# A planned attention and gated-FFN kernel: fillers, transfer rates and the order of the work set anew

## The chip, the cores and the metric

One core of a Trainium2 chip runs the whole program. The metric is the device time of one execution in microseconds (us), from start to end, as the median of several runs. The core has a matrix engine (TensorE, PE in the profile; PEld is its loading of weights), a vector engine (VectorE, DVE), a scalar engine (ScalarE, ACT), a general engine (GpSimd, POOL) and a queue for transfers (SyncE, SP). Each takes its instructions in the order of the program and waits at semaphores for the others. Transfers go through 16 DMA engines; they are issued here by GpSimd, SyncE and ScalarE.

## What is computed

Attention without softmax over 8 batches of 12 heads, 448 positions and 64 values a head, and then a gated feed-forward block over the 3584 resulting rows:

```python
scores = scale * np.matmul(q, k.transpose(0, 1, 3, 2))
attn = np.maximum(scores, 0.0) ** 2 / S
attn_out = np.matmul(attn, v)

x = attn_out.transpose(0, 2, 1, 3).reshape(B * S, H * D)   # 3584 x 768
g = x @ w_gate                                             # 768 x 1536
gelu = 0.5 * g * (1.0 + erf(g * inv_sqrt2))
out = (gelu * (x @ w_val)) @ w_out                         # 1536 x 768
```

Inputs and output are float32 in memory; the kernel computes in bfloat16 with float32 sums.

## The kernel before

**Tiles.** TensorE is used as four 64 x 64 quarters. Nearly every product is a matmul of 64 x 64 weights with up to 448 columns, and one instruction of the plan is a pair of them on one half of the rows: the lists `PE0` and `PE1` hold the pairs of the two halves, and both run at the same time. A batch has six pairs of heads, and its work is cut in three thirds of four heads. For a third, `load_qk` brings queries and keys (`qk16`), which are turned: for batches 0 and 1 and one third of batch 2 by transposes on TensorE against a unit matrix `ident` (`add_first_transposes`, `add_transposes`) and a copy to `qkT`, for all others by a transposing DMA from SyncE (`add_dma_transposes`). Then seven score units a third, 21 a batch (`add_scores`): a score product into a PSUM tile `sp` (there are two), relu by ScalarE into `attnT` (line 757), and the square by VectorE (line 766). `add_values` multiplies `attnT` with the values `v16` into a bank `ff`, copied as `xT`. The feed-forward part takes `xT` with the gate and value weights `wg0` to `wg5`, `wv0` to `wv5` (each 256 of the 1536 columns) either plainly (`add_gate_value`) or, for two batches at a time, with sums of tiles and seven products in place of eight (`add_pair`); the result `uT` goes through the output weights `wo`, also with seven products (`add_product`), into `osb`, and from there to memory (`emit_store`).

**Order.** None of the order is left to a scheduler at run time. While the program is built, `run_plan` plays through a model of the engines: every step is an `Op` with a cost, the steps that it depends on, and a `lag`; at each turn the one that can start first is emitted. For TensorE the order is mostly given from outside. The string `LINE` lists the units after the first batch (`s` is a score unit, `o` a value unit, a digit a gate or value product of that batch, three letters like `2F6` a pair product, two like `b2` an output product), `LOADS` lists the loads on GpSimd's queue after the first batch (`w`, `o`, `q`, `v`), and the numbers `SPOTS`, `FIRSTS`, `PLACE5`, `TURNS` and `SOON` set the places of the first batch's steps, which `work` holds with a time each.

**Loads in the plan.** `load` gives each transfer a time, its bytes in float32 by a rate: 300e3 bytes per us for the first batch, 400e3 after it, 385e3 for weights, all times `SLOW` = 1.06, one after the other, landing 2 us after their end. What waits for one waits for a margin as well: `LATE` = 1.0 us for weights and for batches 1 and 2, `LATER_BY` = 3.0 us for all later ones.

**Fillers.** In the first `FILL` = 30 us the function `fill` is told of each stretch in which the plan has TensorE idle. It puts matmuls of 512 columns of a zero tile (`held`, line 611) there, as many as 0.22 us each fit, into a bank `ff` whose last reader is done. A bank that was not yet used at all is not in `held` and is not taken.

**The end.** The last of 14 groups of output rows makes two row tiles, `t0` and `t1`, in halves of 384 columns. The last two stores of whole rows (`t1`) both go to SyncE's queue; the half rows of `t0` go one to SyncE and one to ScalarE each time.

Of the kernel before, what the change touches and what calls it, by code (L numbers as in the profile page):

```python
# [8 lines left out]


LINE = """
b2 0E1 0 s 2F6 1 s 2B1 3 s 2E6 o 1 a7 o s 1 0F7 0 0 2 s s s 0 s 0F1 j6 3 h1 0F3 0E5 0 s 0 o o a2 s
s a4 s o 0 0F5 3 b1 s c1 3 0E2 0 0 c5 2A1 s 0F6 1 o 0 0E7 o s 0 0 2A3 2 1 2E1 2F7 o 1 d4 s 0 2 0 1
s s 2B7 s a6 2B2 s s s 2D6 2B6 2D1 2 6J4 s s 2A2 4 i1 4C1 1 0E4 s 0F4 0 j5 3 o o a1 4D1 1 b3 s o
2B5 1 g2 o 0 0E6 a3 2A5 s s 0 1 s 1 o c6 s 1 0F2 s s s s 1 s 1 2A6 o s 1 0 s 2F1 2D4 1 o s s o 2F3
a5 s 2D2 s s d1 b5 2F5 1 g7 s 1 s 6B4 s 2A7 0E3 s s s 2D3 s s 1 s 4F1 b6 2 2A4 s c7 2 2 s s s s 2C4
d5 4A5 o o b7 c4 s 2 s 2 s s o s 2D7 s c3 h5 2B3 b4 2C1 s 2C2 3 s 5 2B4 4E3 s 4F3 s 4A4 c2 o 2 s
6I6 d7 2C3 s s 2F2 2E7 2D5 4E1 s s k3 s o o 3 s 2C5 d6 s 3 s s 4 2E4 6K1 n5 s 6F4 2F4 o h6 2C6 f4 s
s e3 f1 2E2 2C7 s s e6 e2 d3 3 3 4A2 s 4A1 o s 2E3 2 4C3 f7 s 4 e7 s 2E5 e1 4D2 o o s o e4 2 s g6 s
d2 f3 f5 e5 4D4 3 f2 s s s s s g1 6H2 6D1 6D4 3 5 s o 6A4 h3 k7 o 4F2 o 4 4B1 s 4 s o s s 4 6B6 s s  # L20
n4 6J7 4C4 f6 s 4B3 s 4 4D3 s 4F5 g4 s g5 s o 4F6 5 4D6 s s g3 6B7 4A7 s 4E6 4A3 4C2 4 4B5 s 4A6
6D2 s s 4D7 s o o 6E1 4F7 j4 h7 s 4C5 4C7 4B7 4B6 s o 4B2 6I5 s s o 5 s s l6 s 4 j2 4B4 4C6 4 4 s o
6I7 4E2 s l3 s 4D5 4 s m3 s 5 s s 4E7 6L4 s o s 6G1 m7 h2 4E4 6A1 s 4F4 o s o 6D7 5 n3 s 4E5 6J5
6C6 6D5 6A2 s s j1 6L1 s 6A6 s 6H7 5 5 j7 6B1 i7 s 6B2 5 o s 5 6I1 i5 5 6I2 s 6H5 s m4 h4 6B3 s 6D3
5 s s 6G7 s i2 n6 6L7 s i3 s 6E7 6F7 6C5 s i6 m6 s j3 6B5 s s 6E2 6J6 i4 6C1 s 6K6 o 6A7 k1 6K7 6K3
l5 6A5 6G4 6C3 6C7 6J1 6A3 6E3 6E6 6C2 6L2 6H4 6H3 l1 m5 6D6 6C4 6I4 l7 6F3 n1 6G2 6E4 6H1 6L3 k5
6F1 m1 6F2 6G3 6F5 k6 6I3 6K2 m2 6J2 6E5 6L6 6F6 l4 6H6 k4 6G6 6G5 6K4 n7 6K5 6J3 l2 n2 k2 6L5
# [289 lines left out]
def kernel(  # L317
# [10 lines left out]
    nc = tc.nc  # L328
# [5 lines left out]
    B, H, S, D = q.shape  # L334
# [33 lines left out]

    NP = 3
    NP2 = 1  # L370
# [71 lines left out]
    def load(nbytes, emit, deps=(), cost=0.7, rate=400e3):  # L442
        def paced():
            ins = emit()
            for d in op.behind:
                tc.add_manual_dep(ins.ins, d.ins.name, SYNC, reason="pace")
            if turned:
                tc.add_manual_dep(ins.ins, turned[-1].ins.name, SYNC, reason="pace")
            loaded.append(ins)

        op = Op("POOL", cost, paced, deps)
        op.behind = [*deps]
        arrivals[op] = nbytes / rate
        op.margin = LATE if late_loads else 0.0
        POOL.append(op)
        return op

    def load_w12(i):
        cols = slice(i * WCH, (i + 1) * WCH)

        def emit(wt, src):
            return nc.gpsimd.dma_start(
                wt[:, :, :], src[:, cols].rearrange("(c p) f -> p c f", p=128))
        w12_op[i] = [load(4 * d_model * WCH, lambda wt=wt, src=src: emit(wt, src), rate=385e3)
                     for wt, src in ((wg[i], moe_w_gate), (wv[i], moe_w_val))]

    def load_wo(i):
# [6 lines left out]
    def load_qk(b, i, h0, h1, deps=()):  # L474

        src = (q, k)[i]
        m, r0 = divmod(h0, 4)

        def tile_of():
            if (b, m) not in qk16:  # L480
                pool, tag = (lpool, "qkr") if (b, m) in STAGED else (hpool, "qk16")
                qk16[b, m] = pool.tile([128, 4, SC * D], bf16, name="qk16", tag=tag)
            return qk16[b, m][HALF[i], r0:r0 + h1 - h0, :]

        op = load(4 * (h1 - h0) * S * D, lambda: nc.gpsimd.dma_start(  # L485
            tile_of(), src[b, h0:h1].rearrange("h (p c) d -> p h (c d)", c=SC)),
            deps, rate=400e3 if b else 300e3)
        qk_loads.setdefault((b, m), []).append(op)
        for pr in range(h0 // 2, h1 // 2):
            head_op[b, pr, i] = op  # L490

    def load_v(b, h0, h1, deps=()):

        m = h0 // 4
        for i in range(2):
            def emit(i=i):
                if (b, m) not in v16:
                    v16[b, m] = qkv.tile([128, 4, VC, D], bf16, name="v16", tag="v16")
                c0 = i * (SC - VC)
                return nc.gpsimd.dma_start(  # L500
                    v16[b, m][HALF[i], :, :, :],
                    v[b, h0:h1].rearrange("h (p c) d -> p h c d", c=SC)[:, :, c0:c0 + VC, :])
            op = load(4 * (h1 - h0) * VC * P * D, emit, deps, rate=400e3 if b else 300e3)
# [93 lines left out]
    def fill(t0, t1):  # L597

        if t1 > FILL or t0 <= warm_op.end:
            return  # L600
        at_rest = {k: -1.0 if r is None else r.end for k, r in held.items() if r is None or r.end is not None}
        if not at_rest:
            return
        k = min(at_rest, key=lambda k: at_rest[k])
# [1 line left out]
        n = int((t1 - t0 - 0.15) / 0.22)  # L606
        if n < 1:
            return
        t = new_bank(k, held[k])
        for _ in range(n):  # L610
            nc.tensor.matmul(t[:, :], warm[:, 0:128], warm[:, :], start=True, stop=True)  # L611

# [594 lines left out]
    def add_product(at, gr, name, final):  # L1207
# [94 lines left out]
        def emit_store(j, engine=nc.sync, part=slice(0, d_model)):  # L1302
            b, c = chunks[t % 2][j]
            rows = out[b * S:(b + 1) * S, :].rearrange("(p c) d -> c p d", c=SC)
            engine.dma_start(rows[c, :, part], osb[t][HALF[j], part])

        if name in "2345":
            st["done", t] = [*st.get(("done", t), ()), *reads]
            if final and t == t0:
                SP.append(Op("SP", 0.6, lambda: emit_store(0, nc.sync, cols), reads, prio=-1))  # L1310
                ACT.append(Op("ACT", 0.5, lambda: emit_store(1, nc.scalar, cols), reads, prio=-1))
                SP[-1].stored = ACT[-1].stored = 0.25
            elif len(st["done", t]) == 2:
                queues = (SP, "SP", 0.6, nc.sync), (ACT, "ACT", 0.5, nc.scalar)
                if final:
                    queues = queues[:1] * 2
                stored[t] = []
                for j in range(2):
                    (pool, name_, cost, engine), spare = queues[:: -1 if j and gr >= FINAL - 2 else 1]
# [262 lines left out]
```

## Time and profile before

| | us |
|---|---|
| median of 3 runs (397.22 to 400.9) | 399.4 |
| the profiled execution | 401.4 |
| its span, first to last instruction | 399.6 |
| matmuls of TensorE, all shapes (8412), time in which one runs | 389.6 |
| weights loaded into TensorE | 339.9 |
| VectorE busy | 317.6 |
| ScalarE busy | 255.7 |
| GpSimd busy | 95.0 |

A line of the profile names an engine, a line of the kernel, an operation, what it writes and reads (out<-in), a shape, and a count. In lists in order of time the first two numbers are the start and the duration, and the brackets at the end say how long the engine sat idle before it, and what it waited for. In rows by stretches the name of the engine is left out where one was asked for: length, busy time and count, then the TensorE clock that was granted (1.00 is full), the mean share of the DMA engines, and GB/s. Most matmuls are on line 422, a helper, so that they are told apart by their tiles. Line numbers of the changed kernel are 3 to 10 higher.

### The profile page before, as it was taken

The numbers are of one execution on the slowest core, as the hardware profiler recorded it, in microseconds if no ns is written. First come the engines' busy times: TensorE is split into PE (matmuls) and PEld (weight loads), VectorE is DVE, ScalarE is ACT, GpSimd is POOL, SyncE is SP. The second block draws the span as 40 slices with busy tenths as digits, with TensorE's granted clock in tenths as the row PEclk, the third lists the DMA queues.
The fourth block names the chain that finished last, engine by engine and source line by source line (L and its number), as shares of the span: only waits on it lengthen the run. The fifth ranks groups of instructions, "written<-read, shape, count | busy, mean of one in ns | idle before, by whom it ended". The sixth has DMA issues, their size and how long they took to land.

```text
span 399.6 us, 18511 instructions
## 1 busy us (share of the span) xinstructions
PE 389.6 (97%) x8412; PEld 339.9 (85%) x8412; DVE 317.6 (79%) x553; ACT 255.7 (64%) x388; POOL 95.0 (24%) x140
## 2 busy tenths in 40 slices
PE   6999999999999999999999989999999999999994
PEld 2456888888998999899999979999999988778994
DVE  3795896798896687979986778998988898768742
ACT  3876884587887657567667667678877455554310
POOL 8747042052050130310300401311110023631000
PEclk9999999999999999999999999999999999999998
DMA  7999995789698795775769968737623230000046
GB/s 103 194 200 198 197 169 81 124 105 194 97 163 125 125 178 105 99 106 77 90 105 179 147 150 167 108 66 104 75 30 82 62 102 3 3 2 3 23 117 184
DMA packets 75055, 44.39 MB, mean 111 GB/s; under 512 B 34400, under 2 KB 71520, under 8 KB 74976
## 3 DMA queue, kind: packets, MB, share of 16 engines
q0 software_dynamic: 38784, 24.39, 45.0%
q1 hardware_dynamic: 35712, 17.83, 23.2%
q8 instruction: 66, 1.08, 1.1%
q10 hardware_dynamic: 480, 0.98, 0.7%
q14 instruction: 13, 0.11, 0.1%
HBM read 48.76 MB, written 11.01 MB: 150 GB/s over the span
## 4 chain that ended last, share of the span: by engine, by line
PE 96%; DMA 1%; issue 1%; POOL 0%; DVE 0%; ACT 0%; POOLq 0%
PE ff L422 85%; PE sp L422 9%; PE ff L611 1%; DMA qk<-in_k_dram 1%; PE sp L690 1%; PE ff L690 1%; POOL qk L485 0%; DVE osb L1296 0%; ACT osb L1295 0%; POOLq L1566 0%
## 5 line engine op out<-in xcount | busy, mean ns | idle before, releaser
L757 ACT ACTIVATE attnT<-sp 128x896 bf16<-128x896 f32 x168 | 151.9, 920 | 55.0 <-PE sp L422 53.1
L422 PE MATMUL ff<-xT,wg 64*64 64x448 bf16 x1680 | 172.6, 349 | 0.0
L422 PE MATMUL ff<-xT,wv 64*64 64x448 bf16 x1056 | 115.0, 349 | 0.0
L422 PEld LDWEIGHTS <-wv 64*64 64x64 bf16 x1680 | 100.3, 106 | 10.1 <-issue 0.4
L422 PEld LDWEIGHTS <-wg 64*64 64x64 bf16 x1680 | 98.3, 106 | 9.1 <-issue 0.3
L766 DVE TENSOR_TENSOR attnT<-attnT 128x1792 bf16<-128x1792 bf16 (+1 forms) x98 | 92.0, 953 | 11.0 <-ACT attnT L757 10.7
L422 PE MATMUL ff<-attnT,v 64*64 64x448 bf16 (+1 forms) x768 | 84.0, 326 | 1.3 <-issue 1.0
L422 PE MATMUL sp<-qkT 64*64 64x448 bf16 (+1 forms) x768 | 75.1, 330 | 1.2 <-issue 0.6
L422 PEld LDWEIGHTS <-s 64*64 64x64 bf16 x1200 | 71.3, 107 | 1.5
L422 PE MATMUL ff<-ts,wv 64*64 64x448 bf16 x624 | 71.7, 349 | 0.0
L422 PEld LDWEIGHTS <-uT 64*64 64x64 bf16 x912 | 54.8, 107 | 0.9
L500 POOL DMA_DIRECT2D v<-in_v_dram x48 | 29.7, 630 | 108.4 <-DMA qkT<-qkr 41.6
L422 PE MATMUL ff<-ts,ws 64*64 64x448 bf16 x480 | 55.0, 349 | 0.0
L995 DVE TENSOR_TENSOR part<-ff,part 128x448 f32<-128x448 f32 x78 | 47.2, 620 | 8.6 <-PE ff L422 6.2
L422 PEld LDWEIGHTS <-v 64*64 64x64 bf16 x768 | 47.2, 106 | 6.0 <-issue 3.3
L422 PE MATMUL ff<-wo,s 64*64 64x384 bf16 x576 | 52.2, 323 | 0.0
L422 PE MATMUL ff<-wt,s 64*64 64x384 bf16 x624 | 51.4, 322 | 0.0
L422 PE MATMUL ff<-wo,uT 64*64 64x384 bf16 x576 | 51.3, 323 | 0.0
L422 PEld LDWEIGHTS <-ws 64*64 64x64 bf16 x720 | 43.9, 106 | 4.4
L422 PEld LDWEIGHTS <-qkT 64*64 64x64 bf16 x768 | 36.1, 106 | 8.6 <-issue 4.6
L991 ACT COPY part<-ff 128x448 f32<-128x448 f32 x51 | 26.9, 533 | 21.8 <-PE ff L422 20.9
L485 POOL DMA_DIRECT2D qk<-in_q_dram x26 | 16.6, 640 | 98.7 <-ACT attnT L757 48.8
(81 smaller groups left out, 505.5 us busy)
## 6 DMA issues: line engine op xcount, KB each, us to landing
out_dram<-osb SPq DMA_DIRECT2D x50, 192.0 KB, 3.7
v<-in_v_dram POOLq DMA_DIRECT2D x48, 128.0 KB, 5.4
qk<-in_q_dram POOLq DMA_DIRECT2D x22, 224.0 KB, 5.8
qk<-in_k_dram POOLq DMA_DIRECT2D x22, 224.0 KB, 6.3
wg<-in_moe_w_gate_dram POOLq DMA_DIRECT2D x6, 384.0 KB, 10.2
wv<-in_moe_w_val_dram POOLq DMA_DIRECT2D x6, 384.0 KB, 11.3
wo<-in_moe_w_out_dram POOLq DMA_DIRECT2D x8, 288.0 KB, 8.6
out_dram<-osb ACTq DMA_DIRECT2D x4, 192.0 KB, 4.2
```

The costliest lines, as they stand in the source:

```text
L422: return nc.tensor.matmul(o, lhsT, rhs, start=start, stop=stop, skip_group_check=onto, tile_position=(P * row, P * col))
L485: op = load(4 * (h1 - h0) * S * D, lambda: nc.gpsimd.dma_start(tile_of(), src[b, h0:h1].rearrange("h (p c) d -> p h (c d)", c=SC)), deps, ...
L500: return nc.gpsimd.dma_start(v16[b, m][HALF[i], :, :, :], v[b, h0:h1].rearrange("h (p c) d -> p h c d", c=SC)[:, :, c0:c0 + VC, :])
L611: nc.tensor.matmul(t[:, :], warm[:, 0:128], warm[:, :], start=True, stop=True)
L690: nc.tensor.transpose(t[HALF[j], c, :], src[:, 2 * r + j, c, :], ident[:, :], tile_position=(0, P * j))
L757: relu.ins = nc.scalar.activation(duo["a"][:, u % 2, :, :], box[0][:, :, 0:S], AF.Relu).ins
L766: nc.vector.tensor_tensor(a[:, part], a[:, part], a[:, part], op=ALU.mult)
L991: rd.ins = copy(st["t", name][:, :], box[0][:, 0:S]).ins
L995: rd.ins = nc.vector.tensor_tensor(t[:, :], box[0][:, 0:S], t[:, :], op=ALU.add).ins
```

## The change

Nothing that is computed changes. The fillers may use banks that were never used; the plan's rates become 395e3 (first batch and weights) and 405e3 (later batches), `SLOW` becomes 1.0, five of the first transfers get a fixed time on top (`OPENING`), and the margins `LATE` and `LATER_BY` become 0.3 and 1.5. The numbers that place the first batch's steps are new, and a table `SHIFT` moves each step of `work` by some tenths to 4 us (steps of one kind keep their sequence). `TURN` = 2 makes the transposes of batch 1's later thirds come two score units later. `LINE` and `LOADS` are new throughout. Two of the last six stores go to GpSimd's queue: the second half-row store of `t0`'s left half, and the second whole-row store of `t1`.

```diff
 LINE = """
-b2 0E1 0 s 2F6 1 s 2B1 3 s 2E6 o 1 a7 o s 1 0F7 0 0 2 s s s 0 s 0F1 j6 3 h1 0F3 0E5 0 s 0 o o a2 s
+1 o 0 s o c5 0E2 a7 1 b5 s i1 2E2 1 b4 o 0 2A3 s 0E1 4E3 s 2D1 0 0 2D6 1 3 s s 2 o s 0 1 s o s 2 b2
...
 LOADS = """
-w q q w v q v v w w w w v q q o q o q v q v o o q v q v v v v q q v q q v q q v v v q q q q v v q v
+w q w v q v w q w w q v w o q q v o q q v o v v o v q v q q v q q v v q v v q q v q q v q v v q q v
 v v
...
-    AHEAD1, TURN = 0, 0
-    SPOTS = {(0, 4): (-16.7, -16.7, -14.2, -13.8), (0, 5): (-13.9, -13.9, -7.0, -6.9)}
-    FIRSTS = (-14.1, -14.1, -14.1, -14.05, -6.6, -6.2), (-7.3, -7.3, -7.3, -7.2, -6.5, -6.1)
-    TURNS = 0.65
-    SOON = -6.4, -6.3, -6.2
+    AHEAD1 = 0
+    TURN = 2
+    SPOTS = {(0, 4): (-17.83, -15.79, -15.06, -12.73), (0, 5): (-14.08, -12.31, -7.12, -5.64)}
+    FIRSTS = ((-16.99, -13.91, -12.44, -11.94, -6.36, -5.18), (-4.75, -3.17, -2.58, -2.21, -2.2, -2.05))
+    TURNS = 1.55
...
     SPARED = 6
-    LATE = 1.0
-    LATER_BY = 3.0
-    SLOW = 1.06
+    LATE = 0.3
+    LATER_BY = 1.5
+    SLOW = 1.0
+    OPENING = {0: 0.45, 2: 0.5, 3: 0.9, 4: 0.6, 7: 0.45}
...
-        arrivals[op] = nbytes / rate
+        arrivals[op] = nbytes / rate + OPENING.get(len(arrivals), 0.0)
...
-            deps, rate=400e3 if b else 300e3)
+            deps, rate=405e3 if b else 395e3)
...
-        at_rest = {k: -1.0 if r is None else r.end for k, r in held.items() if r is None or r.end is not None}
+        at_rest = {k: -1.0 if held.get(k) is None else held[k].end for k in range(FB)
+                   if held.get(k) is None or held[k].end is not None}
...
-        t = new_bank(k, held[k])
+        t = new_bank(k, held.get(k))
...
-                ACT.append(Op("ACT", 0.5, lambda: emit_store(1, nc.scalar, cols), reads, prio=-1))
-                SP[-1].stored = ACT[-1].stored = 0.25
+                pool, name_, cost, engine = (ACT, "ACT", 0.5, nc.scalar) if name == "3" else (POOL, "POOL", 0.7, nc.gpsimd)
+                pool.append(Op(name_, cost, lambda: emit_store(1, engine, cols), reads, prio=-1))
+                SP[-1].stored = pool[-1].stored = 0.25
...
                 if final:
-                    queues = queues[:1] * 2
+                    queues = queues[0], (POOL, "POOL", 0.7, nc.gpsimd)
...
+    moved = [w[0] + SHIFT.get(n, 0.0) for n, w in enumerate(work)]
+    for kind in {w[2] for w in work}:
+        turns = [n for n, w in enumerate(work) if w[2] is kind]
+        for n, at in zip(turns, sorted(moved[n] for n in turns)):
+            work[n] = (at, *work[n][1:])
     work.sort(key=lambda w: w[:2])
```

More of the change, by code (lines that the diff above doesn't have):

```diff
@@ L17 @@
[L17 to L22, printed above, removed]
@@ new lines @@
+4A1 2F6 4B4 2C6 o 6A6 h1 4B3 4 f3 3 2F2 o s 2E1 4A2 o 2C5 s 2F4 4B1 2E7 o s g2 o 4D6 d5 s s 6C5 d6
+5 3 s 4F6 e3 j4 d3 2C7 s f1 4D3 4E1 s s 6H3 s s s 2 e5 o 2 s d1 2C4 s s s d2 f2 6B7 f6 s s 3 3 4
+4A3 3 d7 o 6J2 4 4F3 s e1 2E3 g1 4A7 s s s s s 4 6K1 6L4 4A6 e4 3 s s s 4C3 h5 4B5 4 6A1 6K7 k7 o s
+f4 s s e2 f7 4F2 6E2 o 5 4 4B7 4D1 s o 4E7 o s s s s 4B6 s k1 s 4 s h3 6G6 o s g4 4A5 o 4D4 6A7 4C2
+s g3 4B2 s o s 4D2 4C6 6D3 6H6 6E6 s 5 4A4 6E3 s s 5 4 6E7 n7 4E2 4D7 s o 6K3 4 6D4 s 6B6 4C4 4F7
+6E1 s s s 4E4 h4 s i3 s 4D5 4C7 4 s 6K2 s 5 s s 4C5 6L7 5 4 6F5 s h7 4E6 s 6A2 j1 5 o o 6B1 h2 6H4
@@ L463, in emit @@
                 wt[:, :, :], src[:, cols].rearrange("(c p) f -> p c f", p=128))
-        w12_op[i] = [load(4 * d_model * WCH, lambda wt=wt, src=src: emit(wt, src), rate=385e3)
+        w12_op[i] = [load(4 * d_model * WCH, lambda wt=wt, src=src: emit(wt, src), rate=395e3)
                      for wt, src in ((wg[i], moe_w_gate), (wv[i], moe_w_val))]
@@ L502, in emit @@
                     v[b, h0:h1].rearrange("h (p c) d -> p h c d", c=SC)[:, :, c0:c0 + VC, :])
-            op = load(4 * (h1 - h0) * VC * P * D, emit, deps, rate=400e3 if b else 300e3)
+            op = load(4 * (h1 - h0) * VC * P * D, emit, deps, rate=405e3 if b else 395e3)
             v_loads.setdefault((b, m), []).append(op)
```

20 lines of the change are left out of this document (11 added, 9 removed).

## The prediction

> **What bounds the kernel now.** I read the page's first and fourth part, then busy time by stretches, then the timelines of the stretch that stood out.
>
> ```profile
> PE 389.6 (97%) x8412; PEld 339.9 (85%) x8412; DVE 317.6 (79%) x553; ACT 255.7 (64%) x388; POOL 95.0 (24%) x140
> 0.00:10.00 10.00, 6.91 (x58) 0.90 0.80 103
> 10.00:20.00 10.00, 10.00 (x134) 0.93 1.39 194
> 20.00:30.00 10.00, 9.80 (x152) 1.00 1.37 200
> 30.00:40.00 10.00, 10.00 (x212) 1.00 1.41 198
> 80.00:90.00 10.00, 10.00 (x226) 1.00 0.88 105
> 313.05 81.55 PE ff L422 x1761
> ```
>
> TensorE is "busy" 97% of the span, but a matmul that waits inside its pipeline counts as busy, so I look at the count in parentheses (matmuls per stretch), not at the busy time. In a settled stretch there are 226 in 10 us; the last 81.55 us hold 1761, 0.046 us each. Against that, the first three stretches hold 58, 134 and 152 (and some of those are idle fillers), which is (226-58)+(226-134)+(226-152) = 334 matmuls of 0.046 us, or 15 us, not done. From 30 us on TensorE is close to its own limit. So an order that does the same matmuls can win only in the first 30 us, in the last store, or at single holes; elsewhere it can only lose. The opening is next.
>
> ```profile
> 6.19 0.57 PE L422 MATMUL sp<-qkT 64*64 64x448 bf16 x8 [0.57 <-ACT qkT L661]
> 7.85 0.81 PE L690 MATMUL ff<-ident,qk 128*64 128x128 bf16 x14 [1.09 <-DMA qk<-in_k_dram]
> 8.59 0.61 PE L611 MATMUL ff<-held 128*128 128x512 bf16 x1
> 9.12 0.59 PE L422 MATMUL sp<-qkT 64*64 64x448 bf16 x4
> 9.64 1.04 PE L611 MATMUL ff<-held 128*128 128x512 bf16 x2
> 10.61 0.59 PE L422 MATMUL sp<-qkT 64*64 64x224 bf16 x8
> 12.67 0.38 PE L422 MATMUL sp<-qkT 64*64 64x448 bf16 x4
> 12.98 0.58 PE L690 MATMUL ff<-ident,qk 128*64 128x128 bf16 x14
> 6.62 1.73 ACT L757 ACTIVATE attnT<-sp 128x896 bf16<-128x896 f32 x2 [0.48 <-PE sp L422]
> 9.77 0.92 ACT L757 ACTIVATE attnT<-sp 128x896 bf16<-128x896 f32 x1 [1.43 <-PE sp L422]
> 11.25 3.60 ACT L757 ACTIVATE attnT<-sp 128x896 bf16<-128x896 f32 x4 [0.56 <-PE sp L422]
> 15.21 2.59 ACT L757 ACTIVATE attnT<-sp 128x896 bf16<-128x896 f32 x3 [0.37 <-PE sp L422]
> 18.19 9.05 ACT L757 ACTIVATE attnT<-sp 128x896 bf16<-128x896 f32 x11 [0.39 <-PE sp L422]
> 32.55 0.92 ACT L757 ACTIVATE attnT<-sp 128x896 bf16<-128x896 f32 x1 [5.31 <-PE sp L422]
> 6.00:8.00 2.00, 0.72 (x14) 1.00 0.95 136
> 8.00:10.00 2.00, 2.00 (x20) 0.51 1.26 173
> 10.00:12.00 2.00, 2.00 (x16) 0.63 1.32 188
> 12.00:14.00 2.00, 2.00 (x29) 1.00 1.32 193
> ```
>
> The first batch hangs on ScalarE: 21 relus, and each needs a score product that TensorE must hand over in its fixed order. Back to back they take 9.05/11 = 0.82 us; in fact they run from 6.62 to 18.19+9.05 = 27.24, 20.62 us for 21 x 0.82 + 0.1 = 17.4 us of work. The missing 3.2 us are the idle times in the brackets (0.37 to 1.43), all put down to TensorE, and all before 18.19. Around them TensorE first sits idle (the transposes at 7.85 wait 1.09 us for a load), then pays twice: the granted clock (the number after the count) falls to 0.51 and 0.63 between 8 and 12 us, so that 14 transposes take 0.81 instead of 0.58; and the fillers, which the plan put behind the transposes in place of the wait, stand ahead of the scores at 9.12 and 10.61 that ScalarE needs.
>
> **The change part by part.** Fillers and opening. The place in TensorE's order is that of the second pair of heads of the first batch: sp are scores, held is the filler's operand, qk16 with ident are transposes. Before, ahead of the transposes and behind them:
>
> ```order
> L422 LDWEIGHTS qkT_203
> L422 MATMUL sp_214<-qkT_203 64x448
> L690 LDWEIGHTS qk16_178
> L690 MATMUL ff_219<-ident_115,qk16_178 64x128
> L690 LDWEIGHTS qk16_178
> ```
>
> ```order
> L690 LDWEIGHTS qk16_178
> L690 MATMUL ff_219<-ident_115,qk16_178 64x128
> L611 LDWEIGHTS held_119
> L611 MATMUL ff_239<-held_119 128x512
> L422 LDWEIGHTS qkT_203
> L422 MATMUL sp_241<-qkT_203 64x448
> ```
>
> Of the changed kernel the same two places:
>
> ```order
> L425 LDWEIGHTS qkT_203
> L425 MATMUL sp_217<-qkT_203 64x448
> L615 LDWEIGHTS held_119
> L615 MATMUL ff_226<-held_119 128x512
> L615 LDWEIGHTS held_119
> L615 MATMUL ff_226<-held_119 128x512
> L615 LDWEIGHTS held_119
> L615 MATMUL ff_226<-held_119 128x512
> L694 LDWEIGHTS qk16_178
> L694 MATMUL ff_230<-ident_115,qk16_178 64x128
> ```
>
> ```order
> L694 LDWEIGHTS qk16_178
> L694 MATMUL ff_230<-ident_115,qk16_178 64x128
> L425 LDWEIGHTS qkT_203
> L425 MATMUL sp_247<-qkT_203 64x448
> L425 LDWEIGHTS qkT_203
> L425 MATMUL sp_247<-qkT_203 64x448
> ```
>
> Three fillers moved from behind a wait into it, and none stands between transposes and scores any more. A filler at full clock is about 0.25 us (an estimate: between 9.64 and 10.61 two took 0.97, mostly at half clock), so three started at 6.76 end near 7.5, still ahead of the load at 7.85; two more, new before the first scores, start at 5.6 and end near 6.1, where the scores waited until 6.19 anyway. So both cost nothing; if the load landed 0.3 us earlier, they would cost what they overhang, some 0.2 us.
>
> The gain, relu by relu, at full clock: transposes 7.85 + 0.58, scores 0.38 (row 12.67) and 0.06 from their end to the relu (9.12 + 0.59 = 9.71, relu at 9.77), so the third relu starts at 8.87 instead of 9.77. The fourth needs the tile copied by VectorE:
>
> ```profile
> 8.69 0.62 DVE L694 COPY qkT<-ff 128x896 bf16<-128x896 bf16 x1 [2.78 <-PE ff L690]
> 25.75 2.22 DVE L766 TENSOR_TENSOR attnT<-attnT 128x896 bf16<-128x896 bf16 x4
> 21.66 0.61 POOL L500 DMA_DIRECT2D v<-in_v_dram  x1 [1.11 <-DMA wv<-in_moe_w_val_dram]
> 23.96 0.61 POOL L485 DMA_DIRECT2D qk<-in_k_dram  x1 [0.50 <-DMA qk<-in_k_dram]
> 29.67 0.90 PE sp L690 x28
> ```
>
> 8.46 + 0.62 + 0.4 of scores = 9.5, so it follows back to back at 9.69 (before 11.25). From there on relus can follow each other as they did after 18.19: the 21 end at 6.62 + 17.4 + 0.53 (the hole that the load leaves) = 24.55, 2.7 us earlier. VectorE sets nearly the same bound: 21 squares, 5 copies and 4 value copies at about 2.22/4 = 0.55 from 8.46 are 16.5 us, to 25.0. Less is left if the eleventh relu waits for its buffer, which comes free with the first values. I take 2.3; the ends are 0.9 (only the first hole) and 2.7.
>
> First order of batch 1 and loads. The 28 transposes of batch 1 stood behind 328 matmuls and start at 29.67; now they stand behind 317. With the 2.3 they come at about 29.67 - 2.3 - 0.5 = 26.9. The loads on GpSimd's queue, between the first query and key of batch 1 (qk16_347, now qk16_370) and the third weights:
>
> ```order
> L485 DMA qk16_347<-in_k_dram 64x4x448
> L485 DMA qk16_429<-in_q_dram 64x4x448
> L485 DMA qk16_429<-in_k_dram 64x4x448
> L462 DMA wg1_140<-in_moe_w_gate_dram 128x6x256
> L462 DMA wv1_146<-in_moe_w_val_dram 128x6x256
> ```
>
> ```order
> L488 DMA qk16_370<-in_k_dram 64x4x448
> L465 DMA wg1_140<-in_moe_w_gate_dram 128x6x256
> L465 DMA wv1_146<-in_moe_w_val_dram 128x6x256
> L503 DMA v16_459<-in_v_dram 64x4x256 x2
> L488 DMA qk16_507<-in_q_dram 64x4x448
> L488 DMA qk16_507<-in_k_dram 64x4x448
> ```
>
> The second query and key (qk16_429, now qk16_507) fell behind two weights and two values.
>
> ```profile
> v<-in_v_dram POOLq DMA_DIRECT2D x48, 128.0 KB, 5.4
> qk<-in_k_dram POOLq DMA_DIRECT2D x22, 224.0 KB, 6.3
> wg<-in_moe_w_gate_dram POOLq DMA_DIRECT2D x6, 384.0 KB, 10.2
> ```
>
> The first key lands just before the issue at 23.96 that waits for it. At 198 GB/s (last number of the row from 30 to 40) two weights of 384 KB take 4.0 us, two values of 128 KB 1.3, query and key of 224 KB 2.3 (KB of 1024 bytes), so the second key lands at 23.8 + 7.6 = 31.4. TensorE reaches those transposes 70 matmuls behind the first 28, at 26.9 + 0.9 + 70 x 0.046 = 31.0. So about 0.4 us of wait; it is the next thing that binds, and it grows with what the opening gains. I take 0.3 as its cost (0 to 0.8), and as much as a gain (0 to 0.8) for the thin stretch before 30 us, since the gate matmuls start earlier there: together 0.
>
> Five copies from VectorE to ScalarE (56 instead of 51 of its kind) cost nothing: ScalarE is busy 64%. The rest of the order holds the same matmuls, save one filler less; I give it 0, between -0.5 and +2 (a wait each at a few places).
>
> Last stores. Two of the last six go to GpSimd's queue.
>
> ```profile
> 394.30 1.87 SPq L1305 DMA_DIRECT2D out_dram<-osb  x1
> 396.26 0.55 SPq L1305 DMA_DIRECT2D out_dram<-osb  x1
> 395.37 0.81 ACTq L1305 DMA_DIRECT2D out_dram<-osb  x1
> ```
>
> SyncE's last store could have gone at 395.4 with ScalarE's but stood behind one that took 1.87 us to issue. GpSimd is idle there, and nothing queues behind its stores. The last store can go up to 0.9 earlier, but the two whole-row stores now follow the last but one product, about 1 us later than before, on the same 16 engines. I take -0.3, between -0.9 and +0.6. [...]
>
> Sum: -2.3 + 0 - 0.3 = -2.6. The profiled execution took 401.4 (span 399.6, 1.8 around it), so its like should take 398.8; the median of the runs shown is 399.4, 2.0 below, so I forecast 396.8.
>
> **The rivals.** (1) More than the opening: the order searched with rates near the measured 198 GB/s also closes thin places after 30 us (212 matmuls against 226 from 30 to 40, 0.6 us) and holes such as these:
>
> ```profile
> 125.31 0.59 issue
> 232.70 1.02 issue
> ```
>
> With 0.6 + 0.9 from the last store and the full 2.7 + 0.8 in the opening: 5.0, or 394.4. Against it: the two holes are put down to issue, to no engine, and another order need not remove them.
>
> (2) The fillers do not hold the clock, or the wait for the second query eats the gain. At half clock the third relu starts at 7.85 + 0.81 + 0.59 + 0.06 = 9.31, 0.44 later than reckoned; two fillers ahead of the fourth relu's scores take twice as long, 0.4 to 0.5; and with a wait for the query of 0.8 instead of 0.3 that is 1.4 off the 2.6: 399.4 - 1.2 = 398.2. For it: between 4 and 8 us TensorE was far from idle, and the clock fell all the same. Against it: the new fillers fill more than 1 us of just that stretch. [...]
>
> (3) Slower: margins. The plan now reckons loads of batches 2 to 7 with 1.5 us and less in reserve where it had 3.0 and 1.0, and TensorE takes its order as it stands: a load that lands late stops everything behind it. Before there were hardly any such waits:
>
> ```profile
> PE ff L690 <- DMA qk<-in_k_dram: 1.1, 1, 1.1
> ```
>
> There are 18 thirds of a batch from batch 2 on, each with loads of its own; 0.4 us late at each is 7.2, and 396.8 + 7.2 = 404.0. It decides from 2.6 us of such waits in all (no gain left) and reads as slower from 6.6. Against it: DMA is far from full after 60 us (105 GB/s at 80 to 90), and the order leaves more room in batch 3: from the scores whose relus pace the loads of its last third to the first scores that use them there are 938 matmuls instead of 842. For it: at the second third of batch 2 there are 804 instead of 872.
>
> **How the numbers follow.** What a measurement here can tell from no change is about 1%, 4 us: faster is below 395.4, slower above 403.4. Forecast as summed 0.53, rival 1 0.22, rival 2 0.13, rival 3 0.12. The forecast's own terms span 399.4 - 2.7 - 0.8 - 0.9 - 0.5 = 394.5 to 399.4 - 0.9 + 0.8 + 0.6 + 2 = 401.9, thin at both ends; about a quarter of it lies below 395.4, which with most of rival 1 makes faster 0.32. Slower is rival 3 but for a little: 0.11. The range from 393.6 to 401.4 leaves out rival 3 and the far ends of rival 1 and of the forecast.
>
> **What would show it.** Right: granted clock 1.00 from 8 to 12 us, three fillers ahead of the second transposes, the third relu near 8.9 and the twenty-first done near 25, over 150 matmuls between 10 and 20 us with fewer fillers. Rival 2: 0.5 in the clock again, or a wait for qk<-in_k_dram near 31 us of over 1 us. Rival 3: waits of TensorE for DMA, or for VectorE's copies behind one, after 80 us. The tail: the last store issued before 396. Wrong altogether: an opening that gains its 2 us and a span that does not get shorter.

## The result, and the profile after

| | before | after |
|---|---|---|
| median of 18 runs each, us | 399.74 (397.22 to 400.90) | 401.06 (399.88 to 403.05) |
| profiled execution, us | 401.4 | 399.88 |
| its span, us | 399.6 | 398.1 |

The ratio is 1.0039, with a 95% interval of 1.0022 to 1.0056: the changed kernel is slower by 0.2 to 0.6%. The ratios are not those of the two medians: they compare all runs of the two kernels, save the few over 1.5% above the fastest of their kernel. The forecast of 396.8 said faster. The two profiled executions say the opposite of the medians, and that is the first thing to notice: the one of before is slower than any of before's 18 runs, and the one of after is the fastest of its 18.

The opening of the changed kernel came out much as the prediction worked it out. The page's busy line, busy time by stretches (length, busy time and matmuls, clock, DMA share, GB/s), then TensorE's and ScalarE's timelines of the changed kernel:

```profile
PE 388.2 (97%) x8411; PEld 338.0 (85%) x8411; DVE 314.6 (79%) x548; ACT 257.6 (65%) x393; POOL 95.6 (24%) x142
0.00:10.00 10.00, 7.94 (x81) 1.00 0.82 108
10.00:20.00 10.00, 9.91 (x166) 1.00 1.36 187
6.55 0.82 PE L615 MATMUL ff<-held 128*128 128x512 bf16 x3
7.58 0.58 PE L694 MATMUL ff<-ident,qk 128*64 128x128 bf16 x14 [0.21 <-DMA qk<-in_k_dram]
8.09 0.38 PE L425 MATMUL sp<-qkT 64*64 64x448 bf16 x4
8.53 15.63 ACT L761 ACTIVATE attnT<-sp 128x896 bf16<-128x896 f32 x19 [0.33 <-PE sp L425]
```

Three fillers stand ahead of the second transposes, the clock is 1.00, the third relu starts at 8.53, and the 19 from there on follow without a gap to 24.16. But a second profiled execution of the kernel before (398.43 us, span 396.6) looks like this in the same place; its ScalarE timeline, then TensorE's stretches:

```profile
8.49 4.30 ACT L757 ACTIVATE attnT<-sp 128x896 bf16<-128x896 f32 x5 [0.29 <-PE sp L422]
13.15 2.59 ACT L757 ACTIVATE attnT<-sp 128x896 bf16<-128x896 f32 x3 [0.37 <-PE sp L422]
16.13 9.05 ACT L757 ACTIVATE attnT<-sp 128x896 bf16<-128x896 f32 x11 [0.39 <-PE sp L422]
8.00:10.00 2.00, 1.85 (x20) 1.00 1.21 160
10.00:12.00 2.00, 2.00 (x30) 1.00 1.18 151
```

No half clock, and the twenty-first relu done at 16.13 + 9.05 = 25.18, not 27.24. So the stretch at half clock on which the prediction built belonged to one execution of before. A third profile with before's opening (the kernel below with only its last stores moved) agrees: clock 1.00 from 8 to 12 us, the twenty-first relu done at 25.67. In both, the pause ahead of the third relu is 0.3 us instead of 1.4, though the old fillers still stand between the transposes and the scores. And after 30 us the changed kernel has waits that before did not have. TensorE's waits by what ended them (us in total, times, longest), first of the changed kernel's profiled execution, then of a second one (403.66 us):

```profile
PE sp L425 <- DMA qkT<-qkr: 1.0, 1, 1.0
PE ff L425 <- DVE part L999: 0.6, 1, 0.6
```

```profile
PE ff L425 <- DMA v<-in_v_dram: 2.1, 1, 2.1
PE sp L425 <- DMA qkT<-qkr: 1.5, 1, 1.5
```

Since busy time hides what is lost inside a stretch (of after's second execution TensorE is busy 2.00 us of 2.00 from 86 to 88 with 52 matmuls and from 92 to 94 with 28), I count TensorE's loss: the length of a stretch less what its matmuls need. A 64 x 64 quarter with 448 columns is put at 0.0467 us, an estimate: at half clock, behind 92 us in the second execution of after, four of them start every 0.373 us, and half of a quarter of that is 0.0467 (at full clock the densest stretches show 0.0472). Other shapes go in proportion, fillers count nothing, and the sum is 362.8 us in all four profiles.

| profiled execution | us | loss 0 to 30 | 30 to 70 | 70 to last matmul | last matmul to end of span |
|---|---|---|---|---|---|
| before | 401.4 | 18.6 | 5.2 | 8.0 | 5.0 |
| before, second | 398.43 | 17.2 | 4.5 | 7.2 | 4.9 |
| after | 399.88 | 16.8 | 3.6 | 9.3 | 5.7 |
| after, second | 403.66 | 17.2 | 3.3 | 13.0 | 5.7 |

Against the second execution of before, the changed kernel gains 0.4 + 0.9 up to 70 us and loses 2.1 after it and 0.8 at the end. Before rounding that is 1.5, the difference of the spans (398.1 - 396.6).

### The profile page after: what moved, and what is told of

It is laid out like the page before. It is cut to its first block, busy times and chain, and to the rows that moved or that the text cites. A ratio compares the mean times of both kernels' runs of the same rounds, so it can differ in the third digit from the quotient of the medians.

```text
span 398.1 us, 18508 instructions
## 1 busy us (share of the span) xinstructions
PE 388.2 (97%) x8411; PEld 338.0 (85%) x8411; DVE 314.6 (79%) x548; ACT 257.6 (65%) x393; POOL 95.6 (24%) x142
## 3 DMA queue, kind: packets, MB, share of 16 engines
q1 hardware_dynamic: 35632, 17.64, 24.9%
## 4 chain that ended last, share of the span: by engine, by line
PE 93%; DMA 2%; ACT 1%; DVE 1%; SPq 1%; issue 1%; POOL 0%; DVEq 0%; POOLq 0%
PE ff L425 83%; PE sp L425 8%; DMA qkT<-qkr 1%; DMA qk<-in_k_dram 1%; PE sp L694 1%; ACT attnT L761 1%; SPq L1309 1%; PE ff L615 1%; POOL qk L488 0%; PE ff L694 0%; DVE attnT L908 0%; DVE part L999 0%; DVE wv L908 0%; DVE osb L1283 0%; ACT xT L844 0%
## 5 line engine op out<-in xcount | busy, mean ns | idle before, releaser
L425 PE MATMUL ff<-xT,wg 64*64 64x448 bf16 x1680 | 178.0, 349 | 0.6 <-DVE part L999 0.6
L425 PE MATMUL ff<-xT,wv 64*64 64x448 bf16 x1056 | 118.6, 349 | 0.2 <-issue 0.2
L425 PE MATMUL ff<-attnT,v 64*64 64x448 bf16 (+1 forms) x768 | 86.3, 326 | 0.2
L425 PEld LDWEIGHTS <-s 64*64 64x64 bf16 x1200 | 69.1, 107 | 3.5
L425 PE MATMUL ff<-wt,s 64*64 64x384 bf16 x624 | 57.1, 323 | 0.0
L425 PE MATMUL ff<-wo,s 64*64 64x384 bf16 x576 | 54.9, 322 | 0.0
L425 PEld LDWEIGHTS <-uT 64*64 64x64 bf16 x912 | 51.9, 107 | 2.7 <-issue 0.8
L425 PE MATMUL ff<-wo,uT 64*64 64x384 bf16 x576 | 47.4, 323 | 0.0
L995 ACT COPY part<-ff 128x448 f32<-128x448 f32 x56 | 29.4, 534 | 22.3 <-PE ff L425 19.1
L1084 DVE TENSOR_TENSOR uT<-gel,ff 128x448 bf16<-128x448 bf16 x44 | 27.2, 618 | 13.6 <-PE ff L425 11.4
```

The costliest lines, as they stand in the source:

```text
L425: return nc.tensor.matmul(o, lhsT, rhs, start=start, stop=stop, skip_group_check=onto, tile_position=(P * row, P * col))
L995: rd.ins = copy(st["t", name][:, :], box[0][:, 0:S]).ins
L1084: u_op[b, fc].ins = nc.vector.tensor_tensor(uT[b][:, fc, :], gel.pop((b, fc))[:, :], box[0][:, 0:S], op=ALU.mult).ins
```

## The experiments

Theory A: the opening gains about as much as it can, and the new order gives it back at a few late spots of its own. Theory C: the loss lies in the tail, with GpSimd as the last to issue. Others stand in the expectations. Ratios are to the kernel before, measured beside it. First the two kernels again: the changed one with 12 more runs and a second profile, and before with a second profile.

> The changed kernel as it is, for a second profile beside the first (span 398.1, its fastest execution). Theory A (the opening gains its 3 us in every execution, and something later gives it back, more in a usual execution than in the one profiled): about 401.1 us, ratio 1.004; the opening again ends its 21 relus near 24.2 us, and one or more waits of TensorE of over 1 us appear after 60 us that add up to 1 us more than in the first profile. Theory B (the gain in the opening is itself only in some executions): the relus end 1 us or more later than 24.2.

> The kernel before as it is, for a second profile. Theory B1 (the stretch of half clock from 8 to 12 us belonged to the profiled execution, 401.4 against a median of 399.7): granted clock 1.00 throughout the opening, the 21 relus done at about 26 us instead of 27.2, span near 398. Rival (the half clock is there in most executions): 0.5 again between 8 and 12 us and relus done near 27.2.

400.95 (399.87 to 405.58), ratio 1.0065 (1.0028 to 1.0101); and 398.43. Slower again, with single runs of up to 405. The relus end at 24.55, so theory A holds against B. The rows above are from these two.

### The tail

One kernel is the changed one with the last stores by before's queues, the other before with only these two stores moved:

```diff
-                pool, name_, cost, engine = (ACT, "ACT", 0.5, nc.scalar) if name == "3" else (POOL, "POOL", 0.7, nc.gpsimd)
+                pool, name_, cost, engine = (ACT, "ACT", 0.5, nc.scalar)
...
-                    queues = queues[0], (POOL, "POOL", 0.7, nc.gpsimd)
+                    queues = queues[:1] * 2
```

> The changed kernel with its last six stores on the queues of before (SyncE and ScalarE); the order of every other instruction is the same. Theory C (GpSimd's stores cost time at the end: in the profile GpSimd's last DRAIN runs to 397.34 though the last store landed at 396.06): 0.8 to 1.0 us faster than the changed kernel, about 400.2, ratio 1.0015 to 1.002; the program ends about 1.2 us after the last landing instead of 2.0. Rival (SyncE's queue blocks again, as at 394.30 before, 1.87 us to issue one store): no faster than the changed kernel, last landing 0.5 to 1 us later.

> The kernel before with the two stores on GpSimd's queue and nothing else of the change. Theory C: 0.4 to 0.9 us slower than before, ratio 1.001 to 1.0025, with a DRAIN of GpSimd that ends 1.2 us or more after the last landing. My forecast for the tail: 0.3 us faster, ratio 0.999.

After with before's stores: 400.21 (399.09 to 402.13), ratio 1.0026 (0.9998 to 1.0054), 0.7 us below the changed kernel measured beside it. Before with GpSimd's stores: 401.0 (398.73 to 403.92), ratio 1.0042 (1.0007 to 1.0077). The first difference is not clear by itself (the intervals overlap); the second is, though it may be anything from 0.3 to 3.1 us. Both point the same way, and the profile names the cause. GpSimd's closing instructions (count, shortest / median / longest in ns, start of the first and of the last), of the changed kernel, of before with GpSimd's stores, of before's second execution, and of a version with the old stores that comes below:

```profile
L1587 POOLq DRAIN  x3: 46/93/5200, 392.1 to 397.8; - x3
```

```profile
L1578 POOLq DRAIN  x3: 46/102/5356, 391.5 to 397.3; - x3
```

```profile
L1577 POOLq DRAIN  x3: 45/102/5155, 362.9 to 396.3; - x3
```

```profile
L1587 POOLq DRAIN  x3: 46/93/4850, 362.7 to 395.5; - x3
```

GpSimd's queue ends with a drain of 4.8 to 5.4 us in these profiles, whether a store is under way or not. Before, it began at 362.9, when GpSimd had no more to do, and was hidden. In the changed kernel it begins at 392.1 and ends at 397.3. All stores have landed by 396.06, but the closing exchange of the engines, which takes the last 0.8 us, starts only behind the drain. So the span ends 2.05 us after the last landing, against 1.17 in before's second execution. SyncE's last store did go early (its five from 387.60 were all issued by 393.7), as the prediction had it, and GpSimd's two stores landed 3.4 and 3.2 us after their issue, SyncE's last three 2.6 to 3.4, so slower landings of GpSimd's stores are not the cause.

From the last matmul to the end of the span it is 6.4 us in before with GpSimd's stores, against 4.9 in before's second execution. In the new order the two stores cost less: 5.7 with them, 5.3 to 5.4 in the three kernels with the old stores. The rest of the changed kernel's 0.8 at the end stays with the new order.

### Late values loads

Three kernels change the plan's inputs, one the table of loads and one the plan's precedence; the third has both and the old stores:

```diff
-w q w v q v w q w w q v w o q q v o q q v o v v o v q v q q v q q v v q v v q q v q q v q v v q q v
+w q w v q v w q w w q v w o v q q o q q v o v v o v q v q q v q q v v q v v q q v q q v q v v q q v
...
-                          [copy], lag=5.0) for c0, c1 in ((0, VC), (VC, SC))]
+                          [copy], lag=5.0, prio=-2) for c0, c1 in ((0, VC), (VC, SC))]
```

> The changed kernel with one step moved: the values load of batch 2's first third is issued ahead of the two query loads that stood before it in the order of loads. Theory A (the order found anew has late spots of its own in the rest of the kernel, of which the late values load near 88 us is one): no wait of PE for the values load, the clock stays at 1.00 from 80 to 100 us (it fell to half at 91.6 to 95.0 in one of three profiles), median 0.5 to 1.5 us below the changed kernel's 401.0, and no run above 403. Rival C (the loss lies in the tail, two last stores by GpSimd, alone): same median as the changed kernel within 0.4 us, whatever becomes of the wait.

> The changed kernel with the DMA transposes of queries and keys given precedence over stores in the plan, so that near 140 us they no longer stand behind six stores on SyncE's queue. Theory A (late spots): the wait of PE for the transposed queries and keys (1.0 and 1.5 us in two profiles) goes, PE loses at most 0.5 us near 140 us, median 0.7 to 1.5 us below the changed kernel's 401.0; stores move later, which could cost some tenths elsewhere. Rival C (tail alone): within 0.4 us of 401.0.

> The changed kernel with three repairs together: values load of batch 2 first, transposes ahead of stores, last stores by SyncE and ScalarE as before. Theory A: the gains add up to some 2 to 3 us, 397.6 to 399.0, at or below before. Rival C (tail alone): 400.2 as with the stores alone. Rival D (each wait that is taken away only shows the next one, since PE is close to full): 399.8 to 400.6.

Values first: 399.21 (398.49 to 401.01), ratio 1.0000 (0.9974 to 1.0027): theory A's case. The other two missed: 405.53, ratio 1.016, and 403.27, ratio 1.0102. The wait for the transposed queries at 140 us was gone in both, but the precedence made the plan reorder TensorE's work as well, and with it came a new wait near 186 us. TensorE's wait, and the stretch behind it, of the kernel with transposes first:

```profile
PE ff L425 <- DVE part L999: 2.1, 1, 2.1
188.00:190.00 2.00, 2.00 (x27) 0.50 0.86 164
```

So a change of the plan's input can test the whole new order and not the spot. The next kernels hold the order and move single instructions in it. For the loads: in the changed kernel, the two values loads near 58 us are issued ahead of four query and key loads, and no other engine's order changes.

```diff
-        op.emit()
+        kept.append(op) if e == "POOL" and op in arrivals and 47.9 < t < 57 else op.emit()
...
-        last = max(last, op.end)
+        last = [kept.pop(0).emit() for _ in range(len(kept)) if e == "POOL" and 57.8 < t < 58] and op.end or max(last, op.end)
```

> The changed kernel with the two loads of values that stood behind four query and key loads near 58 us issued ahead of them; the other engines' orders stay as they were, so nothing but the loads moves. If the late loads near 88 us carry the spread and most of the 1.7 us: no wait of PE for a load near 88 us, the transposes near 70 us start about 1 us earlier, no half clock at 91 us, median 0.7 to 1.5 us below the changed kernel (ratio 0.9995 to 1.002), the slowest runs under 403; the hole near 326 us stays at 1.2 us. Rival (the wait near 326 us carried it): median within 0.4 us of the changed kernel.

399.22 (398.83 to 400.75), ratio 1.0007 (0.9988 to 1.0026), against 1.0039 and 1.0065 of the changed kernel in other measurements: 1.3 to 2.3 us, and the narrowest spread of all. The chain behind it, in the order SyncE's transposes, GpSimd's next loads, for the changed kernel, for its second execution with what follows there, and for this kernel:

```profile
68.97 5.89 SPq L535 DMA_TRANSPOSE qkT<-qkr  x4
77.60 0.64 POOL L488 DMA_DIRECT2D qk<-in_q_dram  x1 [15.80 <-ACT gel L1079]
```

```profile
70.16 6.11 SPq L535 DMA_TRANSPOSE qkT<-qkr  x4
80.20 0.64 POOL L488 DMA_DIRECT2D qk<-in_q_dram  x1 [18.21 <-DVE attnT L770]
82.63 7.96 DMA v<-in_v_dram
90.64 0.38 PE L425 MATMUL ff<-attnT,v 64*64 64x448 bf16 x2 [2.11 <-DMA v<-in_v_dram]
90.00:92.00 2.00, 1.36 (x28) 0.89 1.34 207
92.00:94.00 2.00, 2.00 (x28) 0.50 1.41 189
94.00:96.00 2.00, 2.00 (x36) 0.75 1.37 199
```

```profile
67.78 6.35 SPq L535 DMA_TRANSPOSE qkT<-qkr  x4
76.44 0.64 POOL L488 DMA_DIRECT2D qk<-in_q_dram  x1 [15.16 <-ACT xT L844]
80.00:90.00 10.00, 10.00 (x226) 1.00 1.18 160
90.00:100.00 10.00, 10.00 (x232) 1.00 0.89 138
```

The code lets transposes and loads take turns: a transpose waits for the last load issued, a load for the last transpose. In the trace the last load of the 58 us group lands at 68.88 and the transposes start at 68.97; the last transpose lands at 76.70 and the loads go on at 77.60 (the releaser named in the brackets only came at the same moment). In the second execution the same two landings are at 70.07 and 79.30, so everything behind is 2.6 us later; the values land at 90.59, TensorE stands for 2.11, and then the clock falls to half: (0.11 x 2 + 0.50 x 2 + 0.25 x 2) / 0.5 = 3.4 us of it. The 2.1 us of wait and the 1.7 lost at half clock are most of the 4.3 us of loss between 80 and 100. With two loads less in that group the chain starts 1.2 us earlier and has room for its jitter.

But this is not the whole of the 1.3 to 2.3. The half clock near 91 shows in one of the five profiles that keep the changed kernel's order of loads and of matmuls (its own two, the old stores, no fillers, and the sums below). And the hole near 326 us, which the expectation had staying at 1.2 us, was gone. TensorE's stretch there, in the changed kernel and in this one:

```profile
320.00:330.00 10.00, 9.38 (x195) 1.00 0.03 6
320.00:330.00 10.00, 10.00 (x216) 1.00 0.08 21
```

The loss from 320 to 340 us is 1.4 in four of those five profiles (in the fifth the sums there are moved) and 0.3 in this kernel and in the one with values first. So in the profiles about 1.0 of the gain lies at that spot, and the late load may explain the single long runs, but hardly the median. How the 1.3 to 2.3 divide between the two is not shown.

### Stores ahead of a transpose

The kernel with values first in the table of loads (399.21, ratio 1.0000), its order held, and the second half of one transpose ahead of six stores on SyncE's queue:

```diff
-        op.emit()
+        kept.append(op) if op.stored and e == "SP" and 128.7 < t < 132.3 else op.emit()
...
-        last = max(last, op.end)
+        last = [x.emit() for x in kept if op.queued and 132.3 < t < 132.4] and op.end or max(last, op.end)
```

> The kernel with the values load moved (399.2 us, ratio 1.000), and in it one thing alone: the second half of one DMA transpose (near 138 us on SyncE's queue) goes ahead of the six stores that stood before it; all other engines' orders are the same to the last instruction. Theory A (late spots of the new order cost their wait each): PE's wait of 1.3 us for the transposed queries and keys goes, PE's loss from 140 to 150 us falls from 1.65 to under 0.5 us, and the median falls by 1.0 to 1.4 us, to about 0.997 of before. Rival D (the wait is taken up again by a later wait, since the loads and transposes that follow set the pace): the hole at 140 goes, another of like size opens before 200 us, median within 0.4 us of 399.2.

397.78 (397.15 to 399.89), ratio 0.9969 (0.9943 to 0.9996): 0.3% below the kernel it was made from, or 1.2 us (measured apart, the intervals overlap). The chain of waits of the changed kernel (start, duration, what), with its stretch, then SyncE's queue and the same stretch of this one:

```profile
136.22 0.87 SPq L1309
137.14 0.89 SPq L1309
138.08 0.77 SPq L1309
138.90 4.43 DMA qkT<-qkr
143.46 0.38 PE sp L425 x4
140.00:150.00 10.00, 9.03 (x196) 1.00 0.78 136
```

```profile
132.34 3.23 SPq L535 DMA_TRANSPOSE qkT<-qkr  x2
135.68 4.35 SPq L1309 DMA_DIRECT2D out_dram<-osb  x6
140.00:150.00 10.00, 10.00 (x221) 1.00 0.85 146
```

The stores still take 4.35 us to issue, but nobody waits for them. 196 matmuls in the stretch became 221, and no wait of its size opened later (loss from 70 us to the last matmul: 6.2, against 7.7 of the kernel it was made from).

The same with the last stores back on SyncE and ScalarE:

> The kernel of the held stores with the last stores back on SyncE and ScalarE as before; nothing else differs. Theory C (GpSimd as the last issuer ends the run late): tail from the last matmul to the end of the span falls from about 5.7 to about 5.2 us, median 0.3 to 0.8 us below the kernel with the held stores, about 0.995 of before. Rival: the tail is as long whoever issues, within 0.2 us of the kernel with the held stores.

397.35 (396.35 to 398.50), ratio 0.9947 (0.9924 to 0.9970): faster than both kernels, 2.1 us below before. Its drain is the row above that begins at 362.7.

### A wait for VectorE

Near 326 us VectorE's pair sums (line 908) run beside GpSimd's multiplications. VectorE, GpSimd and TensorE of the changed kernel, then VectorE and GpSimd of the one with the values loads ahead:

```profile
321.27 0.55 DVE L908 TENSOR_TENSOR attnT<-wg,attnT 128x768 bf16<-128x768 bf16 x1
323.54 1.36 DVE L908 TENSOR_TENSOR wv<-wg,wv 128x768 bf16<-128x768 bf16 x1
324.83 0.61 DVE L999 TENSOR_TENSOR part<-ff,part 128x448 f32<-128x448 f32 x1
325.36 1.35 DVE L908 TENSOR_TENSOR attnT<-wv 128x768 bf16<-128x768 bf16 x1
323.45 1.04 POOL L1008 TENSOR_TENSOR uT<-gel,part 128x448 bf16<-128x448 bf16 x1 [30.66 <-DVE part L999]
325.25 2.35 POOL L1008 TENSOR_TENSOR uT<-gel,part 128x448 bf16<-128x448 bf16 x2 [0.77 <-ACT gel L1003]
327.29 0.38 PE L425 MATMUL ff<-xT,wg 64*64 64x448 bf16 x2 [0.62 <-DVE part L999]
```

```profile
325.56 0.54 DVE L908 TENSOR_TENSOR attnT<-wv 128x768 bf16<-128x768 bf16 x1
326.03 0.61 DVE L999 TENSOR_TENSOR part<-ff,part 128x448 f32<-128x448 f32 x1
325.75 3.57 POOL L1008 TENSOR_TENSOR uT<-gel,part 128x448 bf16<-128x448 bf16 x3 [1.06 <-ACT gel L1003]
```

A sum takes 0.55 alone and 1.36 when it begins just behind a multiplication's start; the additions of line 999, which read one operand from PSUM, take 0.61 in both cases. Both slow sums end 0.41 to 0.42 us after the multiplication beside which they began, the first having taken 0.81 longer than a sum alone; why the one holds up the other is not shown. In the second kernel the same order ran a little shifted: the sum at 325.56 began before the multiplication at 325.75, took 0.54, and TensorE did not wait. To price the spot, two sums go one place later in the changed kernel's order, nothing else:

```diff
-        op.emit()
+        kept.append(op) if e == "DVE" and op.prio == 3 and (320.4 < t < 320.5 or 321.5 < t < 321.6) else op.emit()
```

> The changed kernel with two pair sums of VectorE near 325 us each one place later, behind the addition that PE waits for; nothing else moves. If the slow sums (1.36 us each beside GpSimd's multiplications, 0.55 us elsewhere) hold up that addition: PE's wait of 0.6 us for it goes, PE's loss from 320 to 330 us falls from 1.2 to under 0.6 us, and the median falls by 0.6 to 1.1 us. Rival (the sums are needed at once themselves, so another wait takes the place): loss from 320 to 340 us unchanged, median within 0.4 us.

400.40 (399.00 to 401.92), ratio 1.0032 (1.0010 to 1.0053). The loss from 320 to 330 us fell from 1.2 to 0.75 and the wait from 0.6 to 0.2, less than expected; the median cannot be told from the changed kernel's. So this move wins at most half of the 1.0 us that the spot costs, and whether the spot opens depends on the moment at which the multiplications fall.

### Fillers and orders

Both kernels without fillers in the first 30 us (`FILL` = 0), and the changed kernel with before's `LINE`, `LOADS` and last stores:

> The changed kernel without any filling matmul in the first 30 us (the sixteen or so of the start stay); the plan's order is otherwise the same. If the fillers hold the clock in the opening, as the prediction says: a stretch at half clock shows between 8 and 25 us, the 21st relu is done at 26 us or later (24.2 with the fillers), and the median is 2 us or more above the changed kernel's. Rival (the work itself is dense enough, or the clock drops anyway): within 0.5 us of it.

> The kernel before without its filling matmuls in the first 30 us, its order otherwise the same. If before's own fillers already held the clock in most of its executions, so that the half-clock stretch of its first profiled execution was that execution's own: it gets slower by 1.5 us or more, with a stretch at half clock between 8 and 25 us. If before's fillers landed at the wrong places and did little, as the prediction took it: within 0.7 us of before.

> The changed kernel with before's tables of order and of loads, and the last stores by before's queues: what is left of the change is the filling matmuls and the plan's rates. Theory A (the new order carries the loss): faster than before, 0.3 to 1.2 us below it (398.0 to 399.0 where before has 399.3), with PE's loss from 70 to 390 us near before's 5.8 to 7.2 us. Rival B (fillers and rates carry the loss themselves, since the plan's other rates move work too): at or above the changed kernel with before's last stores, 400.2 or more.

Without fillers, after: 402.76 (398.85 to 405.83), ratio 1.0067 (1.0031 to 1.0104); before: 400.21 (397.28 to 403.58), ratio 1.0010 (0.9982 to 1.0038). TensorE of after without them, with ScalarE's last group of relus, then TensorE's stretches of before without them:

```profile
7.56 0.96 PE L694 MATMUL ff<-ident,qk 128*64 128x128 bf16 x14
13.51 12.32 ACT L761 ACTIVATE attnT<-sp 128x896 bf16<-128x896 f32 x15 [0.49 <-PE sp L425]
```

```profile
12.00:14.00 2.00, 1.86 (x16) 0.51 1.29 192
14.00:16.00 2.00, 2.00 (x30) 0.50 1.43 194
```

The transposes take 0.96 instead of 0.58, and eight score products at 6.61 take 0.96 instead of 0.57: TensorE runs slower there, though the clock column reads 1.00. Eight score products from 12.87 take 0.79, so the rate goes up near 13.4 (an estimate from these three durations). The relus end at 13.51 + 12.32 = 25.83 instead of 24.16, and in before at 27.23 instead of 25.18. So fillers help to bring the clock up and to hold it in both kernels, but not alike: with before's the clock fell in one of three profiles, with the new ones in none of eleven between 8 and 90 us. What the run gains by them is far less than the 2 and 1.5 us expected and is not clear of noise: 0.1 to 1.1 us in after (ratio 1.0067 less 1.0065 or 1.0039, intervals overlapping), 0.4 in before (an interval that holds 1).

The old order with the new rates: 410.94 (408.52 to 412.90), ratio 1.0293 (1.0251 to 1.0336), on rival B's side, but 11 us is far more than either expectation had in mind, and it isn't spread over the rates or fillers: TensorE loses 20.3 us between 70 us and its last matmul. Nor is it evidence on the old order, which does 399.4 with its own numbers. The plan makes each engine's order from the tables and its rates together, and the tables fit one set of rates.

## Why the prediction was wrong

**The step that failed: the way from the profiled 401.4 to the median.** I took off 2.6 for the change, and then 2.0 more because the median of the runs shown lay 2.0 below the profiled execution. But the profiled execution stood so high mainly because of its slow opening, which ended 27.24 - 25.18 = 2.1 us later than that of the second execution (1.4 by TensorE's loss to 30 us). The term of the opening was read from that same stretch, so the stretch was subtracted twice.

**The opening, -2.3.** The rows of the changed kernel came out nearly as reckoned: third relu 8.53 (8.87 reckoned), the last 24.16 (24.55), clock 1.00, fillers inside the wait. The size was right only against the execution that it was read from, 27.24 - 24.16 = 3.1. Against before's second execution it is 25.18 - 24.16 = 1.0, and ten other profiles of the new opening end at 24.1 to 24.9. From the start of the first relu, which itself moves by 0.9 us, the 21 relus take 17.5 to 17.7 us in all eleven, and 18.7 and 18.8 in the two profiles of before's opening without half clock. The first hole, 0.9 of the 2.3, was hardly there to be won: ahead of the third relu those two profiles pause 0.29 and 0.34, the new opening 0.17 to 0.33. What is won is mainly the two later pauses of 0.37 and 0.39. A reading was off besides: the idle times in the brackets add up to 2.75, not 3.2; the rest is that a relu takes 0.92 alone and 0.82 in a row, so that each of the four pauses costs another 0.1.

**Loads of batch 1, 0.** TensorE waits for no load near 31 us, so the wait of 0.3 did not come. The loss from 30 to 70 is 0.9 and 1.3 less than in before's second execution: a gain that the sum put at nothing.

**The rest of the order, 0 (-0.5 to +2).** This is what turned the sign. It was put at 0 because the order holds the same matmuls; the runs showed new waits. Moving the values loads ahead won 1.3 to 2.3, of which about 1.0 goes with the wait for VectorE near 326 us, and moving the stores from ahead of a transpose near 140 us won 1.2. Rival 3 had the mechanism in part, loads that land late; it set 0.4 us at each of 18 places, and the waits were 1.0 to 1.5 near 140 and once 2.1 near 88. Whether the narrower margins let them in wasn't tried by themselves. The issue time of SyncE's stores was not in my sum at all: the plan reckons 0.6 each, and in the row of six they took up to 0.89.

**Last stores, -0.3.** Wrong sign: 0.4 (397.78 to 397.35, measured together) to 0.7 the other way by the medians. The last store went out earlier, as said; what I did not reckon with is that the program ends with GpSimd's drain. That row was in the trace of before, hidden: there it begins at 365.8.

**Five copies to ScalarE, 0.** Nothing speaks against it.

Put together, 1.3 gained up to 70 us (both profiles of after against before's second) against 1.3 to 2.3, 1.2 and 0.4 to 0.7 lost gives 1.6 to 2.9 slower; measured were 1.6 (0.39%) and 2.6 (0.65%). The terms come from different measurements with overlapping intervals, so this is a rough sum. With the values loads, the six stores and the last stores moved the change is worth 2.1 us (397.35 against 399.44; by the ratio 1.2 to 3.0). That this is near the forecast's 2.6 is luck: the opening gave about 1.0 and not 2.3, some 1 us came between 30 and 70, which the sum put at nothing, and the last stores are before's again.

## What to carry to other kernels

Before a gain is read off one profiled execution, compare that execution's time with the runs: where it is above them all, the very stretch that looks worst may be what makes it so, and the way from its time to the median must not take that stretch off again. An order that is planned ahead should leave room where loads and transposes take turns, since their jitter adds up along the chain (here the transposes near 70 us began 1.2 us later in one execution of after than in the other, and the loads behind them 2.6), and should be tested by moving single instructions in it, because a change of the plan's inputs can give another order altogether.

## What was not expected of the hardware

- A wait of about 2 us in the middle of a full kernel cost nearly twice its length: behind 2.1 us near 88, 1.8 and 2.1 near 185 (the two kernels with transposes first) and 2.2 near 144 (after without fillers) the clock was at half for 3.4 us each time, in which half of the work, 1.7 us, is lost. The waits of 1.0 to 1.5 near 140 did not bring it down (1.00 from 140 to 150 us in after with 1.0; a mean of 0.997 or 0.998 over the span, as in after, in three kernels with 1.2 to 1.5), but in the old order with the new rates one of 1.0 in a thin stretch did (325.2 to 328.6).
- GpSimd's drain at the end of this program took 4.8 to 5.4 us, also when its queue had nothing more to do (4.85 from 362.7 on).
- A store that SyncE issues in 0.5 us took up to 0.9 in a row of six.
